# Reordering the opening of a random-feature attention and gated-convolution kernel: filter folded later, basis and filter rows loaded ahead of the transposes, v split behind the first features

## Chip, cores and metric

One core of one Trainium2 chip. The metric is the device time of one execution in microseconds (us), the median over several executions. Most executions of one kernel agree within 0.3 to 1%. A run is called slow when it is over 1.5% above the fastest of its kernel. Ratios below are the mean time of one kernel's fast runs over that of the other's fast runs of the same rounds, so they are not quite the ratio of the medians quoted beside them.

## The reference, cut to what matters

```python
# attention with random features, per batch and head: m = 128, d = 64, s = 576, 8 batches, 8 heads
phi = lambda x: concat([cos(x @ omega.T), sin(x @ omega.T)]) / sqrt(m)
kv, z = phi(k).T @ v, phi(k).sum(0)
attn = (phi(q) @ kv) / (phi(q) @ z)          # den kept away from zero
# gated convolution on x = attn with heads side by side, [576, 512] per batch
x1, x2, x3 = split(x @ w_proj, 3)
x2c = irfft(rfft(x2, axis=seq) * rfft(filter_fft, axis=seq))   # circular convolution along seq
out = (x1 * x2c * x3) @ w_out
```

## The kernel before

The kernel is software-pipelined: while TensorE does the projection, spectrum and inverse of batch b-1 ("filter part"), the features, sums and divisions of batch b run in four head pairs. A pair's last step on VectorE, its strip, copies its turned result into xT, from which the filter part starts. A tracing framework orders each engine's queue by program order and its own estimate of readiness; the queues then run strictly in order.

Batch 0's keys and queries are turned on TensorE. Those of every later batch go a longer way: GpSimd issues element-wise copies that cast to 16 bit and rearrange in DRAM (kD, ktD, qD), and SyncE then issues DMA transposes of the copies (kT, ktT, qT).

```python
def turned_loads(self, b):
    ...
    nc.gpsimd.dma_start(kD.rearrange("(h x y) c -> h x (y c)", h=H, x=16),
                        self.k[b, :, :512, :].rearrange("h (x y) d -> h x (y d)", x=16))
    nc.gpsimd.dma_start(qD.rearrange("s (h d) -> s h d", h=H), self.q[b].rearrange("h s d -> s h d"))
    ...
    nc.sync.dma_start_transpose(out=ktT, in_=ktD)
    nc.sync.dma_start_transpose(out=kT, in_=kD)
    nc.sync.dma_start_transpose(out=qT, in_=qD)
```

The filter needs its own spectrum once: its rows (f) are loaded, folded by six VectorE additions (ff) and multiplied by the basis (fwd).

```python
for c, rows in enumerate(FROWS):
    f = mo.tile([128, 2, DM], FP32, name=f"f{c}", tag=f"tc{c % 2}", bufs=2)
    for p, odd, lo, n in rows:
        self.late(nc.sync.dma_start(f[p:p+n], halves[lo:lo+n]), self.marks["k", 0, 0])
        nc.vector.tensor_tensor(ff[p:p+n, c], f[p:p+n, 0], f[p:p+n, 1], ALU.subtract if odd else ALU.add)
```

v is split into a high part (vh, ScalarE) and a low part (vl, a GpSimd subtraction). The program's frame:

```python
self.loads(0); self.buffers()
for hp in range(4): self.v_split(0, hp)
self.front(0, 0)                       # tail, key and query features of pair 0
for b in range(B + 1):
    for hp in range(4):
        if b < B: self.pair(b, hp)     # next features, sums, division, strips; loads(1) in pair (0, 0)
        if b:     self.hyena(b - 1, hp)
    if b == 0: self.weights()          # weights, basis, filter rows, folds, filter spectrum
```

Of the kernel before, what the change touches and what calls it, by code (L numbers as in the profile page):

```python
# [9 lines left out]
FP32 = mybir.dt.float32  # L10
FP16 = mybir.dt.float16
# [3 lines left out]
ALU = mybir.AluOpType  # L15
# [5 lines left out]
DM = H * D  # L21
NC = 5
# [11 lines left out]
FROWS = [  # L34
    [(0, 0, 0, 128)], [(0, 0, 128, 128)], [(0, 0, 256, 32), (32, 1, 0, 32)], [(0, 1, 32, 128)], [(0, 1, 160, 128)]
]
GRP = [(0, 1, 2), (0, 1, 2), (2, 3, 4), (2, 3, 4), (0, 1, 2, 3, 4), (0, 1, 2, 3, 4)]
QW = 4 * S


def split_np(x):
    h = x.astype(np.float16)
    lo = (x - h.astype(np.float32)).astype(np.float16)
    return h, lo


def _basis():

    n = np.arange(HS)[:, None]
    j = np.arange(NJ)[None, :]  # L50
    ae = 2.0 * np.pi * ((2 * j * n) % S) / S
    ao = 2.0 * np.pi * (((2 * j + 1) * n) % S) / S
    nyq = (1.0 - 2.0 * (n[:, 0] % 2))
    ere, eim = np.cos(ae), -np.sin(ae)
    eim[:, 0] = nyq
    return ere, eim, np.cos(ao), -np.sin(ao)


def _rows(e, o):

    t = np.zeros((128, e.shape[1]))
    t[:32], t[32:64] = e[256:], o[:32]
    return [e[:128], e[128:256], t, o[32:160], o[160:288]]


def _consts():
    ere, eim, ore, oim = _basis()
    z = np.zeros((HS, 128))
    m = slice(0, 128)
    t = slice(128, NJ)  # L70
    z64 = np.zeros((HS, 64))
    mixe = np.concatenate([ere[:, t], eim[:, t], eim[:, t], ere[:, t], z64], 1)
    mixo = np.concatenate([z64, ore[:, t], oim[:, t], oim[:, t], ore[:, t]], 1)
    hme = np.concatenate([ere[:, t], -eim[:, t], ere[:, t], eim[:, t], z64], 1)
    hmo = np.concatenate([z64, ore[:, t], -oim[:, t], ore[:, t], oim[:, t]], 1)
    cols = [(ere[:, m], z), (eim[:, m], z), (z, ore[:, m]), (z, oim[:, m]), (mixe, mixo), (hme, hmo)]
    fwd = np.stack([np.stack(_rows(e, o)) for e, o in cols])
    w = np.full(NJ, 2.0 / S)
    we, wi = w.copy(), w.copy()
    we[0] = wi[0] = 1.0 / S  # L80
    ce, se = (ere * we).T, (eim * wi).T
    co, so = (ore * w).T, (oim * w).T
    zz = np.zeros((64, HS))
    inv = np.stack([
        ce[m], se[m], np.concatenate([ce[t], ce[t], se[t], se[t], zz], 0),
        co[m], so[m], np.concatenate([zz, co[t], co[t], so[t], so[t]], 0),
    ])
    return fwd, inv
# [12 lines left out]
class _Program:  # L101
# [35 lines left out]

    def weights(self):
        nc, cst = self.nc, self.cst
        fwd_np, inv_np = _consts()  # L140
        inv_h, inv_l = split_np(inv_np.transpose(1, 0, 2) * TIS)
        fwd_np = np.ascontiguousarray(fwd_np.transpose(2, 0, 1, 3)).astype(np.float16)
        dr_fwd = nc.inline_tensor(fwd_np, name="fwdc")
        dr_inv_h = nc.inline_tensor(np.ascontiguousarray(inv_h), name="invhc")
        dr_inv_l = nc.inline_tensor(np.ascontiguousarray(inv_l), name="invlc")
        wp = cst.tile([128, 4, 3 * DM], FP16, name="wp", tag="wp")
        nc.gpsimd.dma_start(wp, self.w_proj.rearrange("(c p) n -> p c n", p=128))
        self.wp = [wp[:, c] for c in range(4)]
        self.fwd = cst.tile([128, 6, NC, 128], FP16, name="fwd", tag="fwd")
        self.late(nc.sync.dma_start(self.fwd, dr_fwd.ap()), self.marks["k", 0, 0])  # L150
        ff = self.fold_filter()
        self.inv = []
        for name, dr in (("invh", dr_inv_h), ("invl", dr_inv_l)):
            t = cst.tile([128, 6, HS], FP16, name=name, tag=name)
            self.late(nc.sync.dma_start(t, dr.ap()), self.marks["k", 0, 1])
            self.inv.append(t)
        wo = cst.tile([128, 4, DM], FP16, name="wo", tag="wo")
        with self.tc.issue_after(self.pool_marks["k", 0, 2].ins):
            nc.gpsimd.dma_start(wo, self.w_out.rearrange("(c p) n -> p c n", p=128))
        self.wo = [wo[:, c] for c in range(4)]  # L160
        self.filter_spectrum(ff)

    def late(self, ins, mark):
        self.tc.add_manual_dep(
            ins.ins, mark.ins.name,
            mybir.DependencyInfo(mybir.DependencyClass.Sync, mybir.DependencyReason.DATA), reason="late",
        )

    def fold_filter(self):
        nc, mo = self.nc, self.mo  # L170
        ff = mo.tile([128, NC, DM], FP16, name="ff", tag="x2")
        nc.vector.memset(ff[:, 2], 0.0)
        for c, rows in enumerate(FROWS):
            f = mo.tile([128, 2, DM], FP32, name=f"f{c}", tag=f"tc{c % 2}", bufs=2)
            for p, odd, lo, n in rows:
                halves = self.filt.rearrange("(i n) d -> n i d", i=2)
                self.late(nc.sync.dma_start(f[p : p + n], halves[lo : lo + n]), self.marks["k", 0, 0])
                nc.vector.tensor_tensor(
                    ff[p : p + n, c], f[p : p + n, 0], f[p : p + n, 1], ALU.subtract if odd else ALU.add
                )  # L180
        return ff

    def filter_spectrum(self, ff):
# [200 lines left out]
    def q_features(self, b, g):  # L384

        nc = self.nc
        if g == 0:
            self.qf[b] = self.ft.tile([128, 2, 2, QW], FP16, name=f"qf{b}", tag="qf", bufs=1)
        qf, qT = self.qf[b], self.q_T(b, g)
# [62 lines left out]
    def strip(self, b, hp):  # L452
        nc = self.nc
        if hp == 0:
            self.xT[b] = self.mo.tile([128, 4, S], FP16, name=f"xT{b}", tag="xT", bufs=2)
        xsd = self.xsd.pop((b, hp))
        ps = self.bank([128, S], f"tx{b}_{hp}", FP16)
        for c in range(NC):
            nc.tensor.transpose(ps[:, SOFF[c] : SOFF[c] + 128], xsd[:, c], self.ident)
        nc.vector.tensor_copy(self.xT[b][:, hp], ps)  # L460


    def x2_project(self, b):
# [73 lines left out]
    def run(self):  # L537
        for name in ("vf", "kT", "ktT", "qT", "kf", "kft", "qf", "kvz", "xsd", "xT", "w", "yT", "marks", "pool_marks"):
            setattr(self, name, {})
        self.pools()  # L540
        self.omega_load()
        self.loads(0)
        self.buffers()
        for hp in range(4):
            self.v_split(0, hp)
        self.front(0, 0)
        for b in range(B + 1):
            for hp in range(4):
                if b < B:
                    self.pair(b, hp)  # L550
                if b:
                    self.hyena(b - 1, hp)
            if b == 0:
                self.weights()

    def pair(self, b, hp):
        if hp < 3:
            self.front(b, hp + 1)
        elif b + 1 < B:
            self.front(b + 1, 0)  # L560
        if b == hp == 0:
            with self.tc.issue_after(self.pool_marks["k", 0, 0].ins):
                self.loads(1)
        if hp == 3 and b + 2 < B:
            with self.tc.issue_after(self.pool_marks["k", b, hp].ins):
                self.loads(b + 2)
        self.kv(b, hp)
        if b + 1 < B:
            self.v_split(b + 1, hp)
        self.attend(b, hp)  # L570
        if hp:
            self.strip(b, hp - 1)
        if hp == 3:
            self.strip(b, 3)
# [75 lines left out]
```

## Time and profile before

| | before |
|---|---|
| median of the first three runs | 450.31 us (449.33 to 456.09) |
| span of the profiled run | 450.5 us, mean granted TensorE clock 0.962 |
| busy TensorE, VectorE, ScalarE, GpSimd | 78, 65, 53, 52% of the span |

How to read what follows: in the time-ordered list, each line has start, duration, engine, source line, operation, output and inputs, and in brackets how long the engine stood idle before it and what ended that. In the waits, the three numbers are the total in us, how often, and the longest. The page's slices divide the span by 40.

### The profile page before, as it was taken

To read this page: it belongs to the slowest core of one execution; us is meant where nothing else is said; L and a number is where in the kernel's file an instruction comes from. 1 tells how busy PE (TensorE), PEld (TensorE's weight loads), DVE (VectorE), ACT (ScalarE), POOL (GpSimd) and SP (SyncE) were. 2 spreads that over 40 slices of the span, in tenths; PEclk is the share of its full clock that TensorE was granted. 3 is DMA by queue.
4 is the path that set the end of the run, shared out by engine and by line. 5 is a ranking of instruction groups with operands and counts; after the bars stand their busy time and mean duration, and the time that the engine had idled before them with its cause. 6 is when DMAs were issued, how large, how long until landed. Compare 5 with 4: busy or idle time off the path is not lost.

```text
span 450.5 us, 8997 instructions
## 1 busy us (share of the span) xinstructions
PE 352.6 (78%) x3728; PEld 235.6 (52%) x3728; DVE 293.4 (65%) x517; ACT 236.9 (53%) x300; POOL 234.7 (52%) x204
## 2 busy tenths in 40 slices
PE   1540375689889996999789968996999788998993
PEld 0330262356646674567456755674566645674571
DVE  3813478469884879477954887488749775754550
ACT  3330271893579355935666467735694278322422
POOL 8550174267845585648471956386637553332251
PEclk9999996899989999999699999999799989999998
DMA  9999869906955386538625392529420003001102
GB/s 175 145 193 249 204 130 107 206 7 92 88 133 130 84 54 159 130 83 54 157 83 95 43 158 94 119 48 106 114 99 1 1 1 106 2 1 48 58 1 105
DMA packets 106056, 43.52 MB, mean 97 GB/s; under 512 B 82352, under 2 KB 99248, under 8 KB 105904
## 3 DMA queue, kind: packets, MB, share of 16 engines
q0 software_dynamic: 45024, 11.55, 27.6%
q1 hardware_dynamic: 60992, 31.40, 26.3%
q8 instruction: 29, 0.48, 0.5%
q14 instruction: 11, 0.09, 0.1%
HBM read 36.80 MB, written 17.69 MB: 121 GB/s over the span
## 4 chain that ended last, share of the span: by engine, by line
PE 45%; DVE 24%; ACT 10%; DMA 9%; POOL 7%; issue 4%; SPq 0%; DVEq 0%; ACTq 0%; POOLq 0%
PE xg L94 10%; PE xc L94 8%; PE kv L424 7%; PE x2p L94 7%; DVE tc L484 6%; DMA f<-in_moe_filter_fft_dram 5%; PE op L94 4%; DVE angk L350 3%; PE nd L441 3%; ACT kf L378 3%; POOL yT L522 3%; DVE vth L344 2%; DVE vtl L345 2%; DVE xsd L446 2%; ACT qf L399 2%
## 5 line engine op out<-in xcount | busy, mean ns | idle before, releaser
L378 ACT ACTIVATE kf<-angk 128x2048 f16<-128x2048 int16 x32 | 61.2, 1912 | 35.9 <-POOL angk L351 34.3
L399 ACT ACTIVATE qf<-angq 128x2048 f16<-128x2048 int16 x32 | 60.2, 1906 | 29.5 <-PE nd L441 14.8
L94 PE MATMUL xg<-xT,wp 128*128 128x288 f16 x512 | 71.2, 286 | 5.3 <-DVE cv L521 3.3
L351 POOL TENSOR_SCALAR angk<-angk 128x1024 int32<-128x1024 int32 x32 | 33.8, 1056 | 60.6 <-DVE angk L350 36.7
L522 POOL TENSOR_TENSOR yT<-w,cv 128x576 f16<-128x576 f32 x32 | 45.4, 1420 | 33.2 <-DVE cv L521 24.7
L94 PEld LDWEIGHTS <-wp 128*128 128x128 f16 x512 | 49.6, 98 | 24.1 <-issue 9.5
L350 DVE TENSOR_SCALAR angq<-thq 128x1024 int32<-128x1024 f32 (+1 forms) x40 | 44.5, 1113 | 23.5 <-ACT kf L378 12.5
L485 POOL TENSOR_TENSOR yg<-tc,tc 128x1024 f16<-128x1024 f32 x16 | 37.4, 2356 | 40.6 <-DVE tc L484 40.6
L351 POOL TENSOR_SCALAR angq<-angq 128x1024 int32<-128x1024 int32 (+1 forms) x40 | 40.9, 1022 | 33.4 <-DVE angq L350 33.0
L339 POOL TENSOR_TENSOR vl<-vf,vh 128x512 f16<-128x512 f32 x32 | 37.4, 1178 | 34.8 <-ACT vh L338 33.7
L503 DVE TENSOR_TENSOR w<-xg,w 128x288 f32<-128x288 f32 x64 | 27.9, 452 | 38.6 <-PE xg L94 36.4
L501 ACT ACTIVATE w<-xg 128x288 f32<-128x288 f32 x64 | 25.4, 410 | 51.4 <-PE xg L94 50.3
L424 PEld LDWEIGHTS <-kf 128*128 128x128 f16 x1024 | 45.1, 101 | 7.6 <-issue 3.6
L94 PE MATMUL op<-wo,yT 128*128 128x512 f16 (+1 forms) x160 | 40.2, 381 | 4.6 <-POOL yT L522 4.2
L350 DVE TENSOR_SCALAR angk<-thk 128x1024 int32<-128x1024 f32 x32 | 39.0, 1219 | 6.8 <-ACT qf L399 4.1
L424 PE MATMUL kv<-vh,kf 128*128 128x65 f16 x512 | 39.2, 200 | 1.7 <-ACT kf L378 1.7
L394 PE MATMUL thq<-qT,om 128*128 128x512 f16 x64 | 21.5, 416 | 24.4 <-DVE angk L350 23.3
L441 PE MATMUL nd<-kvz,qf 128*128 128x65 f16 x640 | 27.1, 195 | 16.1 <-DVE kvz L429 10.8
L94 PE MATMUL xc<-invh,yg 128*128 128x288 f16 x128 | 38.5, 317 | 1.1 <-ACT w L501 1.1
L94 PE MATMUL xc<-invl,yg 128*128 128x288 f16 x128 | 38.3, 316 | 0.0
L94 PE MATMUL x2p<-wp,eo 128*128 128x512 f16 x160 | 36.8, 379 | 1.4 <-ACT o L534 1.3
L441 PEld LDWEIGHTS <-qf 128*128 128x128 f16 x640 | 24.7, 98 | 25.2 <-issue 16.9
(89 smaller groups left out, 710.3 us busy)
## 6 DMA issues: line engine op xcount, KB each, us to landing
vf<-in_v_dram SPq DMA_DIRECT2D x16, 512.0 KB, 4.5
out_dram<-o SPq DMA_DIRECT2D x32, 256.0 KB, 2.1
qD<-in_q_dram POOLq DMA_DIRECT2D x7, 576.0 KB, 8.1
kD<-in_k_dram POOLq DMA_DIRECT2D x7, 512.0 KB, 8.4
f<-in_moe_filter_fft_dram SPq DMA_DIRECT2D x4, 512.0 KB, 9.3
wp<-in_moe_w_proj_dram POOLq DMA_DIRECT2D x1, 1536.0 KB, 22.2
vft<-in_v_dram SPq DMA_DIRECT2D x16, 64.0 KB, 5.1
out_dram<-o SPq DMA_DIRECT2D x8, 128.0 KB, 4.6
```

Source lines behind the costliest of these rows:

```text
L94: nc.tensor.matmul(outap, l, r, start=(i == 0), stop=(i == n - 1))
L339: nc.gpsimd.tensor_tensor(self.vl[hp], vp, vh, ALU.subtract)
L350: self.nc.vector.tensor_scalar(t[:, 0], th, TO_PHASE, None, ALU.mult)
L351: self.pool_mark = self.nc.gpsimd.tensor_scalar(t[:, 1], t[:, 0], 1.0, TURN / 4, ALU.mult, ALU.add)
L378: self.marks["k", b, hp] = nc.scalar.activation(kf.rearrange("p t a r m -> p t (a r m)"), ang, AF.Sin, scale=TO_ANGLE)
L399: nc.scalar.activation(qf[:, :, hh, 1024 * g : 1024 * (g + 1)], ang, AF.Sin, scale=TO_ANGLE)
L424: nc.tensor.matmul(ps[:, hh, t, : 1 + D] if i < 5 else ps[:, hh, t, :D], l, r_, start=(i == 0), stop=(i == len(terms) - 1),)
L441: nc.tensor.matmul(ps[:, c], qf[:, t, hh, o : o + 128], kvz[:, hh, t], start=(t == 0), stop=(t == 1))
L484: nc.vector.tensor_tensor(t[i], ps[:, None, :].broadcast_to([128, 2, DM]), hc, ALU.mult)
L485: nc.gpsimd.tensor_tensor(self.yg[g], t[0], t[1], ALU.add)
L503: nc.vector.tensor_tensor(w[:, ns], ps, w[:, ns], ALU.mult)
L522: nc.gpsimd.tensor_tensor(self.yT[b][:, dc], self.w.pop((b, dc)).rearrange("p a s -> p (a s)"), cv.rearrange("p a s -> p (a s)"), ALU.mult,)
```

## The change

Its intent is to take the filter out of the way of batch 0: the folds are put behind the strip of pair 2 on VectorE, the loads are traced early so that they are done by then, and v's splitting no longer stands ahead of the first features. Cut to its core:

```diff
+FTAG = ["tc0", "tc1", "tc1", "tc0", "tc0"]
+FBUFS = {"tc0": 2, "tc1": 2}
 def weights(self):
+    with self.tc.issue_after(self.pool_marks["k", 0, 0].ins):
         nc.gpsimd.dma_start(wp, ...)
     self.late(nc.sync.dma_start(self.fwd, dr_fwd.ap()), self.marks["k", 0, 0])
-    ff = self.fold_filter()
+    self.filter_loads()                       # the loads alone, tags as in FTAG
     ...                                       # inverse basis as before
-    with self.tc.issue_after(self.pool_marks["k", 0, 2].ins):
+    with self.tc.issue_after(self.pool_marks["k", 0, 1].ins):
         nc.gpsimd.dma_start(wo, ...)
-    self.filter_spectrum(ff)
 def fold_filter(self):
+    with self.tc.issue_after(self.marks["strip", 0, 2].ins):
         ...                                   # the memset and six additions
 def run(self):
-    for hp in range(4): self.v_split(0, hp)
     self.front(0, 0)
+    for hp in range(4): self.v_split(0, hp)
     ...
-            if b == 0: self.weights()
+            if b == 0: self.filter_spectrum(self.fold_filter())
 def pair(self, b, hp):
     if b == hp == 0:
         ...                                   # loads(1), as before
+        self.weights()
```

(The diff also repeats the helper `late`, which does nothing new.)

More of the change, by code (lines that the diff above doesn't have):

```diff
@@ L139, in weights @@
         nc, cst = self.nc, self.cst
+        wp = cst.tile([128, 4, 3 * DM], FP16, name="wp", tag="wp")
+        with self.tc.issue_after(self.pool_marks["k", 0, 0].ins):
+            nc.gpsimd.dma_start(wp, self.w_proj.rearrange("(c p) n -> p c n", p=128))
+        self.wp = [wp[:, c] for c in range(4)]
         fwd_np, inv_np = _consts()
@@ L142, in weights @@
         fwd_np = np.ascontiguousarray(fwd_np.transpose(2, 0, 1, 3)).astype(np.float16)
+        self.fwd = cst.tile([128, 6, NC, 128], FP16, name="fwd", tag="fwd")
         dr_fwd = nc.inline_tensor(fwd_np, name="fwdc")
-        dr_inv_h = nc.inline_tensor(np.ascontiguousarray(inv_h), name="invhc")
-        dr_inv_l = nc.inline_tensor(np.ascontiguousarray(inv_l), name="invlc")
-        wp = cst.tile([128, 4, 3 * DM], FP16, name="wp", tag="wp")
-        nc.gpsimd.dma_start(wp, self.w_proj.rearrange("(c p) n -> p c n", p=128))
-        self.wp = [wp[:, c] for c in range(4)]
-        self.fwd = cst.tile([128, 6, NC, 128], FP16, name="fwd", tag="fwd")
         self.late(nc.sync.dma_start(self.fwd, dr_fwd.ap()), self.marks["k", 0, 0])
-        ff = self.fold_filter()
+        self.filter_loads()
         self.inv = []
-        for name, dr in (("invh", dr_inv_h), ("invl", dr_inv_l)):
+        for name, x in (("invh", inv_h), ("invl", inv_l)):
+            dr = nc.inline_tensor(np.ascontiguousarray(x), name=name + "c")
             t = cst.tile([128, 6, HS], FP16, name=name, tag=name)
@@ L167, in late, with filter_loads @@
         )
+    def late(self, ins, mark):
+        self.tc.add_manual_dep(
+            ins.ins, mark.ins.name,
+            mybir.DependencyInfo(mybir.DependencyClass.Sync, mybir.DependencyReason.DATA), reason="late",
+        )
+    def filter_loads(self):
+        nc, mo = self.nc, self.mo
+        halves = self.filt.rearrange("(i n) d -> n i d", i=2)
+        self.fl = []
+        for c, rows in enumerate(FROWS):
+            f = mo.tile([128, 2, DM], FP32, name=f"f{c}", tag=FTAG[c], bufs=FBUFS[FTAG[c]])
+            for p, _, lo, n in rows:
+                self.late(nc.sync.dma_start(f[p : p + n], halves[lo : lo + n]), self.marks["k", 0, 0])
+            self.fl.append(f)
     def fold_filter(self):
@@ L171, in fold_filter @@
         ff = mo.tile([128, NC, DM], FP16, name="ff", tag="x2")
-        nc.vector.memset(ff[:, 2], 0.0)
-        for c, rows in enumerate(FROWS):
-            f = mo.tile([128, 2, DM], FP32, name=f"f{c}", tag=f"tc{c % 2}", bufs=2)
-            for p, odd, lo, n in rows:
-                halves = self.filt.rearrange("(i n) d -> n i d", i=2)
-                self.late(nc.sync.dma_start(f[p : p + n], halves[lo : lo + n]), self.marks["k", 0, 0])
-                nc.vector.tensor_tensor(
-                    ff[p : p + n, c], f[p : p + n, 0], f[p : p + n, 1], ALU.subtract if odd else ALU.add
-                )
+        with self.tc.issue_after(self.marks["strip", 0, 2].ins):
+            nc.vector.memset(ff[:, 2], 0.0)
+            for c, rows in enumerate(FROWS):
+                f = self.fl[c]
+                for p, odd, _, n in rows:
+                    nc.vector.tensor_tensor(
+                        ff[p : p + n, c], f[p : p + n, 0], f[p : p + n, 1], ALU.subtract if odd else ALU.add
+                    )
         return ff
@@ L459, in strip @@
             nc.tensor.transpose(ps[:, SOFF[c] : SOFF[c] + 128], xsd[:, c], self.ident)
-        nc.vector.tensor_copy(self.xT[b][:, hp], ps)
+        self.marks["strip", b, hp] = nc.vector.tensor_copy(self.xT[b][:, hp], ps)
     def x2_project(self, b):
@@ L543, in run @@
         self.buffers()
+        self.front(0, 0)
         for hp in range(4):
             self.v_split(0, hp)
-        self.front(0, 0)
         for b in range(B + 1):
@@ L553, in run @@
             if b == 0:
-                self.weights()
+                self.filter_spectrum(self.fold_filter())
     def pair(self, b, hp):
```

## The prediction

> **What bounds the kernel now.** I read the page's 40 slices first, then the time-ordered list of instructions over the first 100 us, the chain that ended last over the same stretch, the waits of 26 to 52 us, and last the busy times by batch. The slices (11.3 us each) show an opening that is unlike the rest: in the fourth (34 to 45 us) TensorE is at 0 tenths and VectorE at 1, while the DMA engines are at 9 in each of the first four.
>
> ```profile
> PE   1540375689889996999789968996999788998993
> DVE  3813478469884879477954887488749775754550
> DMA  9999869906955386538625392529420003001102
> ```
>
> The waits of 26 to 52 us name the cause, and the list of VectorE's instructions shows it one by one.
>
> ```profile
> DVE ff L178 <- DMA f<-in_moe_filter_fft_dram: 20.1, 5, 8.2
> ...
> 26.48 0.43 DVE L429 TENSOR_SCALAR kvz<-kv 128x260 f16<-128x260 f32 x1 [3.01 <-PE kv L424]
> 34.74 0.69 DVE L178 TENSOR_TENSOR ff<-f 128x512 f16<-128x512 f32 x1 [7.83 <-DMA f<-in_moe_filter_fft_dram]
> 37.11 0.69 DVE L178 TENSOR_TENSOR ff<-f 128x512 f16<-128x512 f32 x1 [1.67 <-DMA f<-in_moe_filter_fft_dram]
> 38.81 0.69 DVE L178 TENSOR_TENSOR ff<-f 128x512 f16<-128x512 f32 x1 [1.01 <-DMA f<-in_moe_filter_fft_dram]
> 40.88 1.39 DVE L178 TENSOR_TENSOR ff<-f 32x512 f16<-32x512 f32 x2 [1.38 <-DMA f<-in_moe_filter_fft_dram]
> 50.47 0.69 DVE L178 TENSOR_TENSOR ff<-f 128x512 f16<-128x512 f32 x1 [8.20 <-DMA f<-in_moe_filter_fft_dram]
> 51.08 1.22 DVE L350 TENSOR_SCALAR angk<-thk 128x1024 int32<-128x1024 f32 x1
> ```
>
> The reader should see that VectorE stands with six folds of the filter at the head of its queue, each waiting for its rows, from 26.9 us to 51.1 us, and that the first instruction behind them (the angles of head pair 1) waits for nothing but them: its matmuls ended at 23.4 us. The division of pair 0 stands behind them too; its numerators were ready at 29.4 us, and it ran at 52.2. The other engines are empty: ScalarE ran nothing from 30.4 to 53.5 us, GpSimd nothing from 28.8 to 52.4. The chain of the opening repeats it, and shows a smaller loss ahead of it:
>
> ```profile
> 9.86 4.57 DVE vth L344
> 14.43 0.02 issue
> 14.46 0.42 DVE vtl L345
> 14.87 0.34 DVE kT L297
> ...
> 26.23 8.48 DMA f<-in_moe_filter_fft_dram
> 34.72 0.02 issue
> 34.74 0.70 DVE ff L178
> 35.44 0.02 issue
> 35.46 5.40 DMA f<-in_moe_filter_fft_dram
> ```
>
> The copy of the first transposed keys (kT) runs at 14.8 us behind a cast of v that took 4.64 us, though its transposes ended at 11.6. From 83 us on the batches are regular, some 47 us each with TensorE busy 41.5 of 47; nothing in the change touches those instructions. So I take the kernel as an opening of about 83 us plus a steady part, and ask only how much the opening shortens.
>
> **What the Trainium skill says.** "Perfetto Trace Analysis", section Per-engine timelines, says that ScalarE, VectorE and GpSimd are strictly first-in first-out. The trace agrees: the ready angles stood for 24 us behind the folds. "SBUF — State Buffer", section SBUF: two separate sides, says that VectorE and GpSimd share a port pair under an exclusive lock, and the loser waits the whole instruction out. The trace agrees: the same cast of v took 4.64 us beside GpSimd's four subtractions of v (9.30 to 13.69 us), and 0.29 us alone at 15.24. "DMA: Bandwidth & Descriptors", section Issuing engines are not separate DMA queues, says that transfers from every queue interleave on the same 16 engines. The trace fits: in the stall the filter rows (SyncE's queue) ran beside the projection weights, which GpSimd had issued and which took 22.2 us. "ScalarE: Activation LUTs", section Table sets, says that cheap functions such as copy are in every set. The trace agrees in that no copy after 10.8 us loads a table; only the first copy (7.27 us) and the first sine (10.76) do, 1.28 us each. With the sine first, one load should go, in time that ScalarE has idle.
>
> **The change part by part.**
>
> Part 1, the folds leave the head of VectorE's queue. They may now be issued only after the strip copy of pair 2, so nothing of the filter is in front of pair 1. Removed: the division of pair 0 goes from 52.2 to about 29.4, that is 22.8 us; ScalarE's next sine, from 53.5 to the end of the last one at 30.4, 23.0 us. Both give **23 us**.
>
> Part 2, v is split behind the first features. The kT copy can follow its transposes: 14.8 minus 11.6, **3.2 us**, through to the first key features. The casts and subtractions don't vanish: 4.4 us on GpSimd, 2.2 on ScalarE, some 1.4 on VectorE uncontended. GpSimd has 3.4 us idle before the first key angles and 2.0 before the first query angles, ScalarE 3.4 and 5.6 us, so they may fit. I keep 3 us. Together 26 us gained.
>
> Part 3, the folds come back later. Six at 0.69 us are 4.2 us, and the memset 0.27 moves with them: 4.5 us. They stand between the strips of batch 0 and the filter's spectrum, where VectorE's output is waited for (the spectrum began at 75.7 us right behind the last strip). So I charge all **4.5 us** to the path.
>
> Part 4, the buffers of the filter rows. One of two buffers of the first tag holds the keys of batch 0 until the transposes of pair 3. Row group 0 takes the other, groups 1 and 2 the second tag, so three groups load early; group 3 takes the keys' buffer, and one group, likely the last, can load only when group 0 has been folded. A 512 KB load took 8.1 to 11.2 us from issue to landing under load. Some 8.2 us less the 3.5 of the other five folds is 4.7 us exposed; the first two spectrum products need groups 0 to 2 alone and take 2.6 us. I charge **3 us**.
>
> Part 5, the batch 1 transposes. The new order puts basis and filter rows ahead of them. They want keys and queries of batch 1 turned by DMA; before, kT was issued at 42.8 us and landed at 52.8 only because the serial filter loads held SyncE's queue. Its features are wanted in pair 3: 66 us before, so 40 us after. By then basis 0.98 MB, three filter groups 0.66, v 1.18, keys and queries written 1.15, turned keys 0.5 and weights 1.5 should have moved, 6.0 MB; at the 240 GB/s of the stall that is 25 us from 15 us on, which ends at 40. So on the edge: I charge **3 us**.
>
> Part 6, a gain I count small. Before, ScalarE ran nothing from 68.4 to 77.2 us, then ten copies of the filter's spectrum (5.1 us), and only then the tail features of batch 1 at 82.3, for which VectorE waited 3.4 us. With the folds later, these features should go ahead of the copies: **3 us** back.
>
> Sum: 26 - 4.5 - 3 - 3 + 3 = 18.5 us. 450.3 minus 18.5 is 432 us.
>
> **The rivals.**
>
> Rival A, the wait is only moved: the opening is bound by DMA. For it: the engines are at 8 or 9 tenths in the first five slices, to 56 us, and everything loaded there is needed by batch 0's filter stage or batch 1. Against it: that stage is not reached before 75 us, the inverse basis is used only near 118 us, and after 57 us DMA falls to 4 to 6 tenths. What matters is which transfer is needed first, and that is kT of batch 1. If it landed no sooner than now, at 53 us instead of 40, 13 us would be lost instead of 3: about 442 us.
>
> Rival B, VectorE stalls again, behind the late fold. The compiler placed the six folds wrongly once, as it took the loads for faster than they are. If the last group's load, issued after the first fold, competes with the turned loads of batches 1 and 2 and takes 11 us, and the next angles stand behind it in the queue, part 4 costs 8 us rather than 3; with part 6 lost too, 440 us.
>
> Rival C, everything fits: transposes on time, the folds and the late load beside the sines of batch 1. Then 26 us and the 3 of part 6 remain less 4 or 5: 425 us.
>
> Rival D, v becomes the wait. The v of batch 1 can load only when that of batch 0 is split, now later and beside the basis and filter rows. ScalarE's cast for batch 1 stands ahead of the query sines (26.2 us). A landing at 30 us would cost some 5 us: 437.
>
> **Range and chances.** Most of the 26 us is idle time of every compute engine behind one queue, and I know of nothing that must fill it wholly; A and B together could leave 8 to 10 us. Hence 423 to 443. Faster by over 2% means under 441.3 us: 0.87. Within 2%: 0.11. Slower: 0.02.
>
> **What would show it.** Right: no wait of VectorE for filter rows before the strip of pair 2; the division of pair 0 at 25 to 28 us; the kT copy near 11.6 us; the tail angles of batch 1 near 41 us (66.7 before); six folds of 0.69 us near 50 us; the spectrum at 52 to 60 us (75.7 before); batches of the same 47 us from there on; one table load. Wrong: DMA waits of over 5 us before the angles of batch 1 (A), over 5 us before the last fold (B), or of the v casts for their load (D), or a steady part that is not shifted whole, which would mean that something besides the opening set its pace.

## The result

The changed kernel takes 478.39 us (477.89 to 481.54, 4 runs) against 450.18 (449.33 to 456.09, 4 runs); the ratio is 1.0648 (95% interval 1.0589 to 1.0707). The profiled run is fast, its span 476.2 us. It is slower by 6.5%, where 4% faster was predicted.

The page's slices of the changed kernel (11.9 us each), of TensorE, VectorE and DMA, then the mean GB/s of each slice:

```profile
PE   1661002457997999699888997999799968997993
DVE  2672001375879577948884578657866876565350
DMA  9699999990396437543854367166820002000202
GB/s 174 91 209 165 96 63 152 149 231 2 57 96 150 123 79 51 151 123 78 59 142 118 84 40 161 68 117 53 164 90 12 1 1 77 26 1 1 99 1 99
```

The hole of the opening has become deeper, not shallower: in two slices TensorE, VectorE, ScalarE and GpSimd are all at 0; in the kernel before, the emptiest slice still had VectorE at 3, with the folds. And the DMA engines are full there (9 tenths) while they move 96 and 63 GB/s. The waits of 20 to 105 us in the changed kernel say for what:

```profile
PEld L391 <- DMA kT<-kD: 34.9, 1, 34.9
PE thk L391 <- DMA kT<-kD: 34.7, 1, 34.7
...
PE thq L410 <- DMA qT<-qD: 12.9, 1, 12.9
...
DVE ff L194 <- DMA f<-in_moe_filter_fft_dram: 1.7, 1, 1.7
```

The 20.1 us wait for filter rows is down to 1.7, as intended. In its place TensorE waits 34.7 us in one piece for the turned keys of batch 1, then 12.9 for the turned queries. The list of VectorE's instructions shows the same moment from the other side:

```profile
26.52 0.25 DVE L461 RECIPROCAL rd<-nd 128x5 f32<-128x5 f32 x2
...
39.09 0.69 DVE L366 TENSOR_SCALAR angt<-tht 128x512 int32<-128x512 f32 x1 [0.59 <-ACT kf L394]
74.40 0.19 DVE L461 RECIPROCAL rd<-nd 128x5 f32<-128x5 f32 x1 [34.62 <-PE nd L457]
```

The division of pair 0 runs at 26.5 us (52.2 before), the tail angles of batch 1 at 39.1 (66.7 before): up to there the opening is over 25 us ahead. Then everything stands, as TensorE's queue has the key matmuls of batch 1 (72.8 us) in front of the numerators of pair 2 (73.6), and its query matmuls (88.3) in front of the sums of pair 3 (89.1). SyncE's and GpSimd's issue lists hold the transfers behind it. Changed kernel:

```profile
23.29 0.63 POOL L278 DMA_DIRECT2D kD<-in_k_dram  x1
...
27.68 2.23 POOL L282 DMA_DIRECT2D qD<-in_q_dram  x1
29.41 1.27 POOL L144 DMA_DIRECT2D wp<-in_moe_w_proj_dram  x1
...
34.11 6.87 SPq L289 DMA_TRANSPOSE kT<-kD  x1
41.08 10.80 SPq L157 DMA_DIRECT2D invh<-invhc  x1
72.26 8.87 SPq L290 DMA_TRANSPOSE qT<-qD  x1
```

The kernel before:

```profile
24.54 2.23 POOL L266 DMA_DIRECT2D qD<-in_q_dram  x1
...
26.23 16.45 SPq L177 DMA_DIRECT2D f<-in_moe_filter_fft_dram  x6
42.79 7.54 SPq L273 DMA_TRANSPOSE kT<-kD  x1
50.42 2.46 SPq L274 DMA_TRANSPOSE qT<-qD  x1
```

kT is issued 8.7 us sooner (34.1 instead of 42.8) and lands 19.9 us later: the view of its tile gives 38.6 us from issue to landing instead of 10.0, so 72.7 instead of 52.8. qD takes 44.6 us instead of 17.2, the projection weights 51.3 instead of 22.2. The DMA views of two windows of 16 us show it in bulk. The queue lines give packets, MB, and the time that their packets took as a share of 16 engines' time (over 100% in sum: packets of both queues are under way on one engine). Changed kernel, 44 to 60 us:

```profile
DMA packets 2412, 1.48 MB, mean 92 GB/s; under 512 B 1944, under 2 KB 2178, under 8 KB 2408
...
q0 software_dynamic: 1207, 1.17, 91.5%
q1 hardware_dynamic: 1205, 0.31, 88.1%
```

Before, 42 to 58 us, with kT, qT, the last filter rows and the end of the projection weights:

```profile
DMA packets 5281, 3.43 MB, mean 214 GB/s; under 512 B 4459, under 2 KB 4459, under 8 KB 5281
...
q1 hardware_dynamic: 4834, 2.11, 51.6%
q0 software_dynamic: 447, 1.32, 41.7%
```

A packet of SyncE's queue (q1, 257 B on average in the changed kernel) took 0.881 x 16 x 16 us / 1205 = 187 ns there, and 27 ns before. The two counts, 1207 and 1205, are nearly equal, as if the queues took turns packet by packet. But the low rate doesn't need equal counts: in a later run (`wo_b2_late`, 52 to 64 us) SyncE's queue had 914 packets and GpSimd's 237, at 54 GB/s.

How the delay runs on: the key matmuls of batch 1 come at 72.8 us (64.3 before), its query matmuls at 88.3 (67.7 before), the folds only behind them on VectorE at 94.1, the filter's spectrum at 103.7 (75.7 before), the first x2 cast of batch 0's filter part at 116.5 (92.0 before). The first x2 casts of batches 1 and 2 are both 22.1 us late, the end 25.7; the 3.6 us between were not traced further.

A rival cause is TensorE's clock: the mean granted clock is 0.889, and 0.962 before. The difference goes with the hole. From 50 to 100 us it is 0.50, while TensorE is busy for 7.7 of the 50 us; from 150 to 450 us, in windows of 50 us, it is 0.90 to 1.00 in the changed kernel and 0.93 to 1.00 before. What the low clock adds right behind the hole was not tested.

### The profile page after: what moved, and what is told of

Same layout as the page of the kernel before. It is cut to its first block, busy times and chain, and to the rows that moved or that the text cites. A ratio compares the mean times of both kernels' runs of the same rounds, so it can differ in the third digit from the quotient of the medians.

```text
span 476.2 us, 9000 instructions
## 1 busy us (share of the span) xinstructions
PE 356.7 (75%) x3728; PEld 238.6 (50%) x3728; DVE 286.9 (60%) x517; ACT 237.5 (50%) x300; POOL 236.0 (50%) x204
## 4 chain that ended last, share of the span: by engine, by line
PE 43%; DVE 20%; DMA 17%; ACT 8%; POOL 7%; issue 5%; DVEq 0%; ACTq 0%; POOLq 0%
PE xg L96 10%; DMA qD<-in_q_dram 9%; PE xc L96 9%; PE x2p L96 7%; PE kv L440 6%; DVE tc L500 5%; PE op L96 4%; DMA qT<-qD 3%; PE nd L457 3%; POOL yT L538 2%; DVE xsd L462 2%; ACT qf L415 2%; DVE vtl L361 2%; ACT kf L394 2%; POOL angq L367 2%
## 5 line engine op out<-in xcount | busy, mean ns | idle before, releaser
L394 ACT ACTIVATE kf<-angk 128x2048 f16<-128x2048 int16 x32 | 61.1, 1908 | 20.1 <-POOL angk L367 18.5
L538 POOL TENSOR_TENSOR yT<-w,cv 128x576 f16<-128x576 f32 x32 | 45.4, 1420 | 33.9 <-DVE cv L537 25.4
L96 PEld LDWEIGHTS <-wp 128*128 128x128 f16 x512 | 49.6, 98 | 24.8 <-issue 10.2
L354 ACT CAST vh<-vf 128x512 f16<-128x512 f32 x32 | 19.5, 617 | 79.4 <-PE kv L440 78.7
L367 POOL TENSOR_SCALAR angk<-angk 128x1024 int32<-128x1024 int32 x32 | 35.1, 1096 | 42.8 <-DVE angk L366 42.7
L367 POOL TENSOR_SCALAR angq<-angq 128x1024 int32<-128x1024 int32 (+1 forms) x40 | 42.0, 1051 | 24.6 <-DVE angq L366 24.1
L391 PE MATMUL thk<-om,kT 128*128 128x256 f16 x128 | 22.9, 293 | 39.6 <-DMA kT<-kD 34.7
L96 PE MATMUL xc<-invh,yg 128*128 128x288 f16 x128 | 40.0, 328 | 1.1 <-ACT w L517 1.1
L440 PE MATMUL kv<-vh,kf 128*128 128x65 f16 x512 | 39.1, 200 | 1.5 <-ACT him L215 1.3
L96 PE MATMUL x2p<-wp,eo 128*128 128x512 f16 x160 | 38.4, 389 | 2.2 <-ACT o L550 1.7
L96 PE MATMUL xc<-invl,yg 128*128 128x288 f16 x128 | 39.9, 326 | 0.0
L457 PE MATMUL nd<-kvz,qf 128*128 128x65 f16 x640 | 28.1, 198 | 14.1 <-DVE kvz L445 11.7
## 6 DMA issues: line engine op xcount, KB each, us to landing
wp<-in_moe_w_proj_dram POOLq DMA_DIRECT2D x1, 1536.0 KB, 51.3
out_dram<-o SPq DMA_DIRECT2D x8, 128.0 KB, 4.4
```

The source lines that it names most:

```text
L96: nc.tensor.matmul(outap, l, r, start=(i == 0), stop=(i == n - 1))
L367: self.pool_mark = self.nc.gpsimd.tensor_scalar(t[:, 1], t[:, 0], 1.0, TURN / 4, ALU.mult, ALU.add)
L394: self.marks["k", b, hp] = nc.scalar.activation(kf.rearrange("p t a r m -> p t (a r m)"), ang, AF.Sin, scale=TO_ANGLE)
L440: nc.tensor.matmul(ps[:, hh, t, : 1 + D] if i < 5 else ps[:, hh, t, :D], l, r_, start=(i == 0), stop=(i == len(terms) - 1),)
L457: nc.tensor.matmul(ps[:, c], qf[:, t, hh, o : o + 128], kvz[:, hh, t], start=(t == 0), stop=(t == 1))
L538: nc.gpsimd.tensor_tensor(self.yT[b][:, dc], self.w.pop((b, dc)).rearrange("p a s -> p (a s)"), cv.rearrange("p a s -> p (a s)"), ALU.mult,)
```

## The experiments

Three events serve as a yardstick throughout: "x2 of batch 0" is the start of the first ScalarE cast of x2 in batch 0's filter part (92.0 us before, 116.5 after); "x2 of batch 1" the same one stage later (141.5, 163.6); "kT" and "qD" are the times from issue to landing for batch 1.

Two theories stood at the start. **Theory 1, overlap**: the transpose kT and the element-wise copies of keys and queries in DRAM slow each other when they run together; before, the serial filter loads happened to hold kT back until qD had landed (41.7 us). **Theory 2, crowd**: GpSimd now has more large transfers under way (qD, both weights, and batch 2's copies), and each waits for all.

### kT behind qD

```diff
+        qd = nc.gpsimd.dma_start(qD..., ...)
+        kt = nc.sync.dma_start_transpose(out=kT, in_=kD)
+        if b == 1: self.late(kt, qd)
```

> The changed kernel, with the one DMA transpose of batch 1's keys (kT) made to wait until the query rows of batch 1 (qD) have landed; every other transfer as in the changed kernel. Theory 1 (overlap): between 41 and 72 us the engines were busy but moved only 60 to 100 GB/s because the transpose ran beside the element-wise copies of qD in DRAM; kept apart, qD lands about 17 us after its issue as in the kernel before (not 44.6), kT within 10 us of its issue (not 38.6), and the time falls to 425 to 445 us. Theory 2 (crowd): the six large transfers issued by GpSimd between 23 and 43 us share the engines, and each waits for all; then qD still takes over 35 us, kT comes even later, and the time stays at 470 us or more.

Measured: 466.47 us (458.70 to 470.02, 6 runs; three of them over the 1.5% limit, with granted clocks of 0.899 to 0.917 where the fast ones had 0.903 to 0.930; the profile is of a slow one). Ratio of the fast runs 1.0158 (1.0046 to 1.027). qD lands in 17.6 us, as Theory 1 says, but kT, issued at 45.4 us, takes 31.9: the copies of batch 2 (issued at 37 to 42 us) are now beside it. Neither theory gets its number; a later run puts both kinds of edit together.

### Batch 2 later, and output weights later too

```diff
-        if hp == 3 and b + 2 < B:                 # loads(b + 2) behind the angles of pair 3
+        if hp == 3 and 0 < b and b + 2 < B:
+        if b == 1 and hp == 0: ... self.loads(2)  # behind the angles of pair (1, 1)
```

The second run issues wo there too.

> The changed kernel with the loads of batch 2 (keys, queries, v) issued about one batch stage later, behind the key angles of pair 1 of batch 1, so that only qD, the projection weights and the output weights are under way beside the kT transpose of batch 1. Theory 2 (crowd): qD lands in under 25 us, the time falls to 430 to 450 us. Theory 1 (overlap of the transpose with qD): qD still runs beside the transpose, takes over 30 us, and the time stays above 455 us.

> As the run with batch 2's loads late, and the output weights (wo) issued there too, so that GpSimd has only qD and the projection weights under way in the opening, as in the kernel before. Theory 2 (crowd): at least as fast as the run with batch 2 late alone, 425 to 445 us. Theory 1 (overlap): no faster than that run by over 5 us, and qD takes over 30 us from issue to landing.

Measured: with batch 2 late 480.5 us (470.20 to 483.61; three of four runs slow, the profiled one too, so no ratio); qD 45.2 us, kT 43.1. With the output weights late too 474.36 us, ratio 1.0504 (1.0429 to 1.0579); qD 38.4, kT 34.9. With no more large copies of GpSimd's under way than the kernel before had, the collapse is there all the same. Theory 2, as a matter of number, falls.

### v alone

```diff
+        self.front(0, 0)
         for hp in range(4):
             self.v_split(0, hp)
-        self.front(0, 0)
```

> The kernel before with one part of the change alone: v of batch 0 is split behind the first features. Both theories: the kT copy runs near 12 us instead of 14.8, and the filter stall of 20 us stays. As the stall is set by the filter loads, which start when the first key features are done, up to 3 us of gain: 446 to 450 us. If GpSimd's subtractions of v then stand in front of the query angles and of batch 1's key loads, the gain is lost: 450 to 453 us.

Measured: 453.83 us, ratio 1.0047 (0.9976 to 1.0118): the same. The filter stall stays (24.5 us of waiting). On its own, with that stall behind it, this part of the change gains nothing. Its cost shows in the changed kernel: GpSimd does the four subtractions of v (4.4 us) right behind the first key angles, and the copies of batch 1 wait behind them. kD is issued at 23.3 us instead of 19.8, qD at 27.7 instead of 24.5.

### Both edits together

> The changed kernel with both edits of the last runs together: kT of batch 1 waits for qD of batch 1, and the loads of batch 2 are issued a stage later, so that no element-wise copy of keys or queries in DRAM is under way while a batch 1 transpose is. Projection and output weights stay beside it. Theory 1, widened by the last runs (any such copy beside a transpose, batch 1's or batch 2's, slows both): kT lands within 12 us of its issue, qT within 8, and the time falls to 425 to 440 us. Theory 2 (crowd): about as the better of the two edits alone, 455 us or more.

> As the run with both edits, with the output weights late too. Theory 1: within 4 us of that run, as the weights' transfers do not slow a transpose (in the kernel before, kT landed in 10.0 us beside the projection weights). Theory 2: clearly faster than it.

Measured: 457.14 us, ratio 1.0096 (0.9991 to 1.0201), and 456.20, ratio 1.0095 (0.9996 to 1.0194). The transfers do as Theory 1 says: kT 12.3 and 10.9 us, qT 6.7 and 5.7. The output weights make no difference. The collapse costs the changed kernel some 21 us, then (medians of different rounds), yet the time is no better than before, 17 us above the 425 to 440 expected. Two reasons show. kT now waits for qD, is issued at 45.0 us and lands at 57.3, later than in the kernel before (52.8). And x2 of batch 0 is at 81.6 us, 10.3 sooner than before, but x2 of batch 1 at 141.7, no sooner: that stage takes 60.0 us instead of 49.6.

### kT early in the kernel before

```diff
-                self.late(nc.sync.dma_start(f[...], ...), self.marks["k", 0, 0])
+                with self.tc.issue_after(self.kt1.ins):      # kt1: kT of batch 1
+                    self.late(nc.sync.dma_start(f[...], ...), self.marks["k", 0, 0])
```

> The kernel before with its filter loads put behind the issue of kT of batch 1 on SyncE's queue, so that kT runs beside qD as in the changed kernel, while the crowd (only kD, qD and projection weights) is that of the kernel before. Theory 1: kT takes over 25 us from issue to landing (10.0 before), qD over 28 (17.2 before), and the kernel slows to 465 us or more. Theory 2: kT lands within 15 us; the time within 5 us of the kernel before, apart from filter rows that come later.

Measured: 456.26 us, ratio 1.0101 (1.0000 to 1.0202). kT takes 21.6 us, twice its time before, but not the 25 of Theory 1, and qD 18.0, hardly slowed. Overlap with qD and the projection weights slows kT, but it is not the collapse.

### The folds alone

```diff
+                with self.tc.issue_after(self.marks["strip", 0, 2].ins):
                     nc.vector.tensor_tensor(ff[...], f[..., 0], f[..., 1], ...)
```

> The kernel before with the folds alone moved behind the strip of pair 2; order of the filter loads, tags, v and weights as before. Theory 1: with the folds late, SyncE's queue holds only three filter loads ahead of kT, so kT is issued before qD lands, or beside batch 2's copies, and is slow: 455 us or more, with kT over 20 us from issue to landing. Theory 2: two things less in the crowd than in the changed kernel (output weights later, v as before), 430 to 445 us.

Measured: 460.83 us, but the four runs are 448.59, 459.92, 461.75 and 463.42; one is fast, so there is no ratio. The profile is of the fast one: kT issued at 34.3 us takes 24.9, TensorE waits 17.6 us for it. So even the part of the change that removes the stall, alone and in its best run, mostly turns it into a wait for kT. What makes one run faster than the other three was not found.

### Fewer, larger packets

```diff
-            qD.rearrange("s (h d) -> s h d", h=H), self.q[b].rearrange("h s d -> s h d")
+            qD.rearrange("(h x) c -> h (x c)", h=H), self.q[b].rearrange("h s d -> h (s d)")   # wrong result
```

> The changed kernel with the query copy in DRAM (qD) written as it is read, in long rows, instead of in pieces of 64 elements; wrong results on purpose (heads and positions are mixed from batch 1 on). Everything else, the crowd and the overlap of kT with it included, is as in the changed kernel. In the collapse the two queues' packet counts were nearly equal in each 6 us window (426 and 425, 447 and 449), some 225 ns for a pair on each engine, however small the packets. If the number of small packets is what costs (the queues take turns, packet by packet), far fewer of qD's remain, qD lands in under 25 us instead of 44.6, kT in under 25 instead of 38.6, and the time falls by 10 us or more. If it is the bytes or the number of transfers under way, qD and kT take over 35 us as before and the time stays at 470 us or more.

Measured: 469.59 us, ratio 1.0385 (1.0325 to 1.0445), some 9 us less than the changed kernel (478.39, measured in other rounds); results wrong, as meant. qD of batch 1 lands in 10.9 us instead of 44.6; kT in 29.4, more than the 25 expected. In this company its small pieces are what counts for qD; for kT the other partners stay. (Batch 2's qD is written in long rows here too.)

### Keys and queries of batch 1 first

If the order of transfers is the bound, turn it round: copies of batch 1 right behind the first key angles, ahead of v's subtractions; basis, filter rows and inverse basis behind qT; both weights behind the angles of pair 3 (`weights()` is traced in pair (0, 2) for that). kT behind qD and batch 2 late are kept.

```diff
         self.front(0, 0)
+        with self.tc.issue_after(self.pool_marks["k", 0, 0].ins):
+            self.turned_loads(1)
         for hp in range(4): self.v_split(0, hp)
-    self.late(... fwd, f: self.marks["k", 0, 0]; inverse basis: self.marks["k", 0, 1])
+    self.late(... all three: self.qt1)          # qT of batch 1
-    wp behind pool_marks["k", 0, 0], wo behind pool_marks["k", 0, 1]
+    wp and wo behind pool_marks["k", 0, 3]
```

> The run with both edits (kT behind qD, batch 2 later) with the order of the opening turned round: key and query copies of batch 1 issued by GpSimd right behind the first key angles, ahead of v's subtractions; basis, filter rows and inverse basis only when qT of batch 1 has landed; projection and output weights behind the angles of pair 3. The question is why taking the collapse away left 457 us. Theory 1 (order): the opening's bound is when kT of batch 1 lands (57 us in that run, 53 in the kernel before), since basis, filter, v and weights are moved ahead of it. Then kT lands at 35 to 42 us, the wait of TensorE for it is under 4 us instead of 17, and the time falls to 425 to 440 us. Theory 2 (volume): everything has to be loaded before batch 0's filter stage anyway; then kT comes early, but TensorE or VectorE waits as long for the weights or the filter rows, and the time stays within 2% of the kernel before.

Measured: 447.25 us, ratio 0.9905 (0.9852 to 0.9957). kT takes 5.4 us and lands at 34.9, and no wait for it is left in the list of waits. x2 of batch 0 is at 74.4 us, 17.5 sooner than before: that is the gain which the prediction had put at 18.5 for the whole. Of it 10.2 us are lost again in the next stage (x2 of batch 1 at 134.2, a stage of 59.7 us). So the signs in the opening are those of its Theory 1, but the time, within 2% of the kernel before, is what its Theory 2 had.

### Batch 2 back in its place, and filter rows in buffers of their own

```diff
-        if b == 1 and hp == 0: ... self.loads(2)
+        if hp == 3 and b + 2 < B: ... self.loads(b + 2)      # as in both kernels
```

The second run adds `FTAG = ["tc0", "tc1", "tc1", "eo", "yT"]`.

> The last version (keys and queries of batch 1 first) with the loads of batch 2 back where the changed kernel has them, as kT and qT of batch 1 have landed (at 35 and 38 us) before these are issued, so nothing can collide. In that version the first stage of batch 0's filter part started 17.5 us sooner than in the kernel before (74.4 against 92.0 us) but the next one only 7.3 us (134.2 against 141.5): a stage of 60 us instead of 50. The run with both edits had the same 60 us, the changed kernel 47, so I take the late batch 2 loads for the cause. Then the stage falls to 47 to 50 us and the time to 432 to 440 us. If the stage stays at 60 us, the cause is another and the time stays near 447 us.

> As that one, with the last two row groups of the filter in buffers of their own (those of two tiles that are not yet in use), so that no filter load waits for a fold or for the keys of batch 0. In the version with keys first, the last load was issued at 53.9 us behind the first fold and took 11.2 us; VectorE waited 4.8 us for it, and the chain of waits counts the 11 us. If that is on the path, 3 to 8 us less than the run without this edit; if the stage behind it is bound by the sines of batch 1 all the same, within 2 us of it.

Measured: 439.62 us, ratio 0.9676 (0.9622 to 0.9730), and 440.00, ratio 0.9702 (0.9647 to 0.9756). The late loads of batch 2 were worth 7.6 us of median (different rounds; the ratios differ by 2.3%); the stage falls to 53.1 us, not to 50. The filter buffers are worth nothing in time. They take away VectorE's wait of 4.8 us for the late load, 11 us long in the chain of waits, and x2 of batch 0 comes at 70.2 us instead of 74.9. But both runs have a new wait, of the cast of v of batch 2 for its load, which SyncE issues behind the transposes: it grows from 2.6 to 7.9 us, and the cast runs at 82.7 instead of 82.2 us.

### Which partner?

From 439.6 us, with kT at 5.1 us and nothing of GpSimd's beside it, the partners were put back one by one.

```diff
 pair_q:   kT no longer waits for qD
 pair_w:   wp issued right behind qD; kT still behind qD
 trio_qw:  both
 trio_qf:  pair_q, with basis and filter rows behind the first key features (ahead of kT)
 quartet:  trio_qf and wp right behind qD
```

> The version with keys first, with kT no longer behind qD: kT runs beside qD alone. If the copies in DRAM alone make the collapse, kT takes over 15 us (5.1 without) and qD over 15 (8.2), and the time rises by 5 us or more from about 440. If qD alone is harmless, kT lands in under 10 us and the time is 436 to 441.

> The version with keys first, with the projection weights issued right behind qD, and kT still behind qD: kT and qT run beside the weights alone. If only the copies in DRAM hurt, kT lands in under 12 us and the time is 436 to 442. If the weights, 22 us long, slow the transposes by themselves, kT takes over 20 us, and the time is 445 or more.

> Both partners: kT beside qD and the projection weights, with no basis or filter rows loading. As in the kernel before with kT early: kT some 20 us. If it is over 30 us, the pair of qD and the weights is enough for the collapse; if 20 or less, basis and filter rows were a part of it in the changed kernel.

> kT beside qD, with basis and filter rows ahead of it on SyncE's queue as in the changed kernel, but weights late. If basis and filter rows are the missing part, kT takes over 25 us; if the weights are, under 15 us.

> The version with keys first, kT free of qD, with all three partners put back: qD, projection weights, and basis and filter rows ahead of kT on SyncE's queue; output weights and batch 2 late. If the partners add up one by one, kT takes 20 to 25 us (5.1 alone, plus 2.9 for qD, 4.7 for the weights, 5.8 for basis and filter), the time some 450 us. If together they collapse as in the changed kernel, kT takes over 30 us and qD over 30, at under 120 GB/s, and the time is over 460.

| kernel | issued to run beside kT | kT, us | qD, us | median, us |
|---|---|---|---|---|
| keys first, batch 2 in place | nothing of GpSimd's | 5.1 | 8.2 | 439.62 |
| pair_q | qD | 8.0 | 8.7 | 443.18 |
| pair_w | projection weights | 9.8 | 8.8 | 446.88 |
| trio_qf | qD, basis, filter | 13.8 | 20.3 | 446.92 |
| trio_qw | qD, projection weights | 14.5 | 8.5 | 450.23 |
| quartet | qD, projection weights, basis, filter | 21.8 | 26.5 | 462.97 |
| changed, wo and batch 2 late | the same, with the inverse basis | 34.9 | 38.4 | 474.36 |
| changed, batch 2 late (a slow run) | and the output weights | 43.1 | 45.2 | 480.5 |
| changed | and batch 2's copies | 38.6 | 44.6 | 478.39 |

kT and qD are from one profiled run each. qD alone does next to nothing, so Theory 1 in its narrow form falls too. No single partner gives the collapse: for kT they about add up, as the expectation for the quartet had it (5.1 + 2.9 + 4.7 + 5.8 is 18.5; 20 to 25 were forecast, 21.8 measured), and qD goes from 8.2 us to 20.3 with basis and filter rows beside it and to 26.5 with the weights too. The sum is no law, though: in the kernel before with kT early, kT took 21.6 us beside qD and the weights, with only the end of the basis and one filter group besides, where trio_qw has 14.5. The DMA view of the quartet has 133 GB/s over 32 to 48 us, that of trio_qw 193 over 24 to 40. From the quartet to the changed kernel kT rises by another 17 us. What the engines do there, packet by packet, no view here shows; that part stays open.

The medians of the table don't follow from kT alone. The quartet is 13 us over the 450 forecast for partners that add up, though its kT landed at 47.5 us, ahead of the kernel before. No wait for kT is in the list of waits of the pairs, trios and quartet from 20 to 105 us. Instead ScalarE waits for v of batch 1, which SyncE issues behind one or both of the slow transposes: 3.9 us in pair_q, 12.6 in pair_w, 13.3 in trio_qf, 15.0 in trio_qw, and in the quartet:

```profile
ACT vh L360 <- DMA vf<-in_v_dram: 28.2, 1, 28.2
```

This is the wait of the prediction's rival D. It isn't in the changed kernel, whose v of batch 1 was issued at 20.2 us and had landed before kT was issued. A transfer that is slowed by its company also holds back those behind it on its queue.

### v of batch 2 ahead of its transposes

```diff
-        self.turned_loads(b); self.v_rows(vf, b); ...
+        self.v_rows(vf, b); ...                       # for batch 2
+        with self.tc.issue_after(self.v_last.ins): self.turned_loads(b)
```

> The version with keys first and batch 2 early, with v of batch 2 loaded ahead of batch 2's transposes on SyncE's queue. In that version the second half of v of batch 2 was issued at 78 us behind the transpose qT, and the chain of waits had 4 to 8 us for it. If that wait is on the path, 433 to 438 us; if the transposes of batch 2 then come late instead, 438 to 443.

Measured: 436.51 us (435.45 to 437.69, 6 runs), ratio 0.9655 (0.9622 to 0.9688), against 0.9676 without the edit: the same within the intervals, with x2 of batch 1 at 125.1 instead of 128.0. (This edit and the filter buffers of their own were not tried together.) This is the fastest version, 3.4% under the kernel before and 8.8% (436.51 over 478.39, from other rounds) under the changed one. The issue list of SyncE's queue shows the difference from the two lists above, with qD issued at 20.8 us, kT landing 5.0 us after its issue, and the filter rows behind both:

```profile
29.55 2.31 SPq L292 DMA_TRANSPOSE kT<-kD  x1
31.92 2.91 SPq L295 DMA_TRANSPOSE qT<-qD  x1
...
36.92 0.34 SPq L151 DMA_DIRECT2D fwd<-fwdc  x1
37.30 3.06 SPq L183 DMA_DIRECT2D f<-in_moe_filter_fft_dram  x5
```

## Why the prediction was wrong

It failed in **part 5**, the batch 1 transposes, and there in one term: "at the 240 GB/s of the stall that is 25 us from 15 us on, which ends at 40". The rate was taken from the kernel before and held constant under another mix of transfers. Measured, it was 178 GB/s from 15 to 40 us and 87 from there to 72.7 us, when kT landed: 33 us later than wanted, where 3 were charged. The volume was not the fault: 7.3 MB moved from 15 us to that landing, and 8.0 MB from 15 us to kT's landing at 52.8 in the kernel before. The company was: with weights, basis and filter rows behind kT and qT, kT landed at 34.9. A slower kernel had been given a chance of 0.02.

Smaller slips of the same part don't change this. The filter groups are 1.31 MB, not 0.66 (two of 512 KB and two pieces of 128 KB), the output weights and the inverse basis were left out, and the stall's mean rate from 26 to 52 us was 216 GB/s, not 240. Two readings of the slices were off too: in the fourth, VectorE is at 3 and not 1, and after 56 us DMA is at 6, 9, 0, 6 and 9 tenths, not at 4 to 6.

**Rival A** named the right wait ("what matters is which transfer is needed first, and that is kT of batch 1"), but its worst case was kT as late as before, 442 us. That kT could come later than before, by being issued sooner, was not considered: the serial filter loads were read as what held kT back, and not also as what kept it apart from the rest.

The other steps, by their own signs:

- **Part 1** was right: the division of pair 0 at 26.5 us (25 to 28 forecast), 25.7 sooner, and the tail angles of batch 1 at 39.1 (41 forecast).
- **Part 2** was wrong in its gain. The kT copy ran at 11.9 us as forecast, but v alone made 1.0047 of the time; the subtractions delayed the copies of batch 1 by 3 us, and in that run kT landed at 57.7 us instead of 52.8. The table load did not go either: the v casts still came first on ScalarE (9.1 us, the first sine at 12.6), so two loads stayed.
- **Part 3** was right in size: six folds and the memset from 93.8 to 99.9 us, with 1.7 of waiting among them. That they cost 4.5 us of time was not tested.
- **Part 4** was too high: 1.7 us of wait in the changed kernel. With keys first the wait was 4.8 us, as the 4.7 of the prediction, but buffers of their own, which took it away, left the time as it was (440.0 against 439.6).
- **Part 6**: the tail features of batch 1 did go ahead of the spectrum's copies (92.7 and 105.8 us), but behind the late kT this says nothing of the 3 us.
- **The steady part shifts whole** held nearly: x2 of batches 0 and 1 and the span are 17.4, 16.5 and 14.8 us ahead of the kernel before in the fastest version.

So the sum of 18.5 us was about right for x2 of batch 0 once keys and queries came first: 17.5 us. That the two agree is partly luck, as part 2 gained nothing alone, part 4 cost nothing and parts 3 and 6 were not tested. The gain was out of reach in the changed kernel, because the transfers that had to be there first were issued among those that could wait.

What the prediction cites on the exclusive lock fits here too: the cast of v, now away from GpSimd's subtractions, took 0.27 us (4.64 before). "DMA: Bandwidth & Descriptors", section Issuing engines are not separate DMA queues, says that transfers interleave on the same engines; the runs agree (the two queues' packets took 91.5% and 88.1% of the engines' time in one window), and add that the total is not conserved when they do (214 and 92 GB/s).

## What to carry to other kernels

When a stall is removed that waited for DMA, ask what the stalled queue had kept apart: list every transfer that will now be under way together and the one that is needed first, and do not carry the old rate over to the new mix. Issue the transfers in the order of their first use, and put a large element-wise copy or a weight load behind a transpose that the next stage waits for, rather than beside it. Moving only the consumers, here the folds, did not pay: the one fast run of the folds alone took 448.6 us, with 17.6 us of waiting for kT.

## What the Trainium skill lacked or had wrong

- "DMA: Bandwidth & Descriptors", section Rules for kernel authors, says that "A transpose next to ordinary DMAs needs nothing". For correctness that holds here; for time it does not: the same transpose took 5.1 us with nothing of GpSimd's beside it, 8.0 to 14.5 beside one or two partners, 21.8 beside three, and 34.9 to 38.6 in the collapse.
- "DMA: Bandwidth & Descriptors", section Issuing engines are not separate DMA queues, has no word on the total: with both queues at work and the engines full (packet times of 93 and 180% of the engines' time in sum), it was 214 GB/s in one window and 92 in another.
- No page has the effect of copy shape on a neighbour: writing qD in long rows brought qD from 44.6 to 10.9 us and kT from 38.6 to 29.4.
